# Attention, a dense MLP and eight routed experts on one core: blocks of 4, 3, 4, 4 and 3 tiles, and an order written out to the end

## The chip, the cores and the metric

One core of a Trainium2 chip. The time is that of one execution of the program on the device, in microseconds (us); lower is better. TensorE is called PE here, VectorE DVE, ScalarE ACT, GpSimd POOL, and SP is SyncE, whose queue issues most of the transfers.

## What is computed

2304 tokens of 512 numbers go through three stages:

```
# 1 attention inside chunks of 64 positions, 8 heads of 64
scores = scale * q_c @ k_c.T ; attn = softmax(scores) ; x = attn @ v_c
# 2 dense MLP, hidden size 2048
h = x @ w_in ; x = (h * clip(h + 3, 0, 6) / 6) @ w_out
# 3 eight experts, hidden size 1024, the two best by a noisy gate
noisy = x @ w_gate + log1p(exp(x @ w_noise)) * noise
top2, top2_w = two largest of noisy, softmax of the two
out[token] = sum over its two experts e:  top2_w * (relu(x @ w1[e]) @ w2[e])
```

Everything is float32. The products of stages 2 and 3 split each operand into a high and a low half and add three products (high by high, high by low, low by high), so every matmul of these stages stands three times.

## The kernel before

A tile is 128 tokens; there are 18. **Blocks.** Stage 2 goes through the tiles in five blocks (BT, 4, 4, 4, 3 and 3 tiles). A block does 16 units of 128 hidden columns. A unit is layer one (`s1`, 12 matmuls, L284, of 128 columns for each tile, into one of two banks), the activation (`mlp_act`: relu with bias on ACT L318, product on DVE L319, copy to the high half on ACT L320; then `mlp_lo`, the low half on DVE, L325), and layer two of the unit before (`mlp_o`, three matmuls, L293, for each tile, added up in one bank for each tile). So PE does layer one of unit u, then layer two of unit u - 1, while ACT and DVE make the halves of unit u.

**Ticks.** Every four matmuls of layer one and every tile of layer two count one tick. Work of other stages is put between matmuls by tick numbers or by unit (`at(...)`).

**Attention and gate beside the blocks.** Attention of block 0's tiles is done first, by itself. The tiles of block b + 1 are attended beside the units of block b: scores (`att_sc`, L187), exponentials, normalization (`att_n`, L225, or in block 0 by head on ACT, L230), transposes (`att_pt`, L237), their copy (`att_at`, L241), the product with the values (`att_xo`, L254), and its halves (`att_hi`, L264, `att_lo`, L267). In block 0 DVE and ACT also convert the MLP's weights from 64-bit words (`conv_1` to `conv_lo`, L152 to L175), two halves of a unit in each of 15 units. Its four attention tiles take four units each; the last is a hurried form (`fast`, three units), which normalizes on DVE. The gate for the tiles of block b - 1 runs beside block b: rows are written to memory, read back and transposed on DVE (L358), multiplied on PE (L399), transposed (L411) and reduced on DVE (L418); then come the best two (`gate_top`, four pieces, L436 to L470), positions in the experts' lists (`gate_pm`, L482, `gate_ps`, L499 to L503), and the scatter of each token's slot on POOL (L506).

**The last block.** For the gates of blocks 3 and 4, whose time is short, `route` uses PE for the transposes too (L382) and puts every step at a tick. Experts work in ten groups: expert 0 in two groups of 3 and 2 tiles, experts 1 to 6 with 5, expert 7 with 3 and 2. Their rows are found in a table (`exp_slots`, L517), gathered by POOL (L541, L557) and transposed: for expert 0 and 1 on PE (`exp_tr`, L567, halves by ACT L569 and DVE L570), later on DVE (`exp_tr_q`), for which the row numbers are worked out first (`exp_index`, DVE, L535, from tq, read from the table and copied three times). The weights of an expert unit are split on ACT and DVE (`split_unit`, L128, L129; called by `pump`, which also loads the unit three later). An expert unit is layer one, relu and low half (L583, L584), and layer two of the unit before (`exp_o`, L293). `exp_y` scales (L599 to L604) and POOL adds the rows to the output (L605). `counts` (L615 to L621) works out the longest list, which PE and others read into a register.

**What sets the order.** Inside `manual_schedule` an engine follows the order in which the program is written. This holds for PE, DVE and ACT up to the end of block 3 and from group 2 to the end; in the last block and groups 0 and 1 it holds for PE alone, and a scheduler places DVE and ACT's work; SP and POOL are placed by it throughout. The last `exp_o` and `exp_y` stand outside. Eight banks hold everything: four accumulators and two for layer one, and a pair, p6 and p7, for the rest (transposes, logits, gathered rows).

## Time and profile before

| | |
|---|---|
| median of 3 runs | 957.58 us (956.69 to 957.6) |
| the profiled execution | 958.57 us, of which the span is 956.8 |
| mean granted clock of PE | 0.989 of full speed |
| PE busy | 925.0 us, 97% of the span |
| DVE, ACT, POOL busy | 487.5, 339.5, 243.3 us (51, 35 and 25%) |

The span is the time from the first to the last instruction in the trace. PE is busy nearly throughout, so idle time of PE, its length and its releaser, is what to look for; busy shares of the other engines say little by themselves. The granted clock is the share of full speed that PE was given; below 1 the same matmuls take longer while PE still counts as busy.

### The profile page before, as it was taken

How to read it: one execution, taken by the hardware profiler on the slowest of the kernel's cores; microseconds unless marked ns; L12 is line 12 of the kernel's file. 1: busy time of each engine (PE TensorE's matmuls, PEld its weight loads, DVE VectorE, ACT ScalarE, POOL GpSimd, SP SyncE). 2: the span in 40 equal slices, each digit the busy share in tenths (PEclk: the TensorE clock that was granted, in tenths of full speed). 3: DMA queues.
4: the chain of work that ended last, by engine and by line, in shares of the span. 5: the costliest groups of instructions: out<-in, count | busy, mean ns of one | idle time of the engine just before them, and what ended most of it. 6: DMA issues, size and time to landing. Idle time of an engine off the chain costs nothing.

```text
span 956.8 us, 14478 instructions
## 1 busy us (share of the span) xinstructions
PE 925.0 (97%) x5810; PEld 785.3 (82%) x5810; DVE 487.5 (51%) x912; ACT 339.5 (35%) x658; POOL 243.3 (25%) x219
## 2 busy tenths in 40 slices
PE   7999899999999999999998999999999999999995
PEld 4677677777777888889987888998989999898894
DVE  6999954445444444555642554544545444441321
ACT  5566433233323333355531433333334333321210
POOL 0000000001100300033004474544746455432311
PEclk8999999999999999999999999999999999999998
DMA  9536431111841160035322753553636354140421
GB/s 348 192 103 207 167 99 55 34 34 51 272 162 34 34 186 2 1 79 164 112 98 57 177 148 116 122 127 95 146 119 133 117 115 127 62 58 20 56 33 26
DMA packets 50940, 102.67 MB, mean 107 GB/s; under 512 B 17200, under 2 KB 23728, under 8 KB 50864
## 3 DMA queue, kind: packets, MB, share of 16 engines
q1 hardware_dynamic: 39312, 80.64, 26.6%
q0 software_dynamic: 11552, 21.02, 11.8%
q8 instruction: 47, 0.77, 0.3%
q14 instruction: 29, 0.24, 0.1%
HBM read 78.31 MB, written 23.28 MB: 106 GB/s over the span
## 4 chain that ended last, share of the span: by engine, by line
PE 75%; DVE 11%; issue 7%; ACT 3%; DMA 2%; POOL 1%; SPq 0%; POOLq 0%; DVEq 0%; ACTq 0%
PE bp L284 36%; PE bp L293 32%; PE pair L293 4%; DVE u L161 2%; DVE u L153 2%; DVE r L319 1%; DVE g L325 1%; DVE w L175 1%; POOL table L506 1%; DVE u L152 1%; PE pair L254 1%; DMA table<-pay,slot 1%; PE pair L187 1%; ACT w L168 1%; PE pair L237 1%
## 5 line engine op out<-in xcount | busy, mean ns | idle before, releaser
L293 PE MATMUL bp<-w,g 128*128 128x512 f32 x1680 | 424.6, 398 | 0.0
L293 PEld LDWEIGHTS bp<-w,g 128*128 128x128 f32 x1680 | 310.4, 189 | 64.8 <-issue 0.8
L284 PE MATMUL bp<-Xa,w 128*128 128x320 f32 (+3 forms) x1344 | 249.0, 336 | 1.0 <-ACT w L168 1.0
L284 PEld LDWEIGHTS bp<-Xa,w 128*128 128x128 f32 x1344 | 215.9, 189 | 23.1 <-ACT w L168 1.8
L541 POOL DMA_INDIRECT xrq<-x2d,iq x120 | 131.7, 1097 | 105.2 <-DVE arena L358 40.3
L506 POOL DMA_INDIRECT table<-pay,slot x36 | 35.4, 982 | 457.7 <-DVE slot L503 448.2
L584 DVE SCALAR_TENSOR_TENSOR g<-bp,g 128x320 fp32r<-128x320 f32 (+2 forms) x128 | 62.8, 491 | 137.5 <-ACT g L583 137.5
L129 DVE TENSOR_TENSOR w<-raw,w 128x1024 fp32r<-128x1024 f32 x64 | 78.5, 1226 | 89.5 <-ACT w L128 89.3
L583 ACT ACTIVATE g<-bp 128x320 fp32r<-128x320 f32 (+2 forms) x128 | 56.0, 438 | 184.1 <-PE bp L284 184.0
L284 PE MATMUL bp<-Xe,w 128*128 128x320 f32 (+1 forms) x672 | 107.0, 314 | 1.0 <-ACT Xe L569 0.7
L284 PEld LDWEIGHTS bp<-Xe,w 128*128 128x128 f32 x672 | 103.5, 188 | 4.2 <-ACT Xe L569 0.9
L284 PE MATMUL bp<-Xb,w 128*128 128x384 f32 (+1 forms) x480 | 105.8, 366 | 0.0
L319 DVE SCALAR_TENSOR_TENSOR r<-r,bp 128x512 f32<-128x512 f32 (+1 forms) x80 | 50.7, 633 | 104.6 <-ACT r L318 104.4
L284 PEld LDWEIGHTS bp<-Xb,w 128*128 128x128 f32 x480 | 85.3, 188 | 12.4 <-issue 1.8
L318 ACT ACTIVATE r<-bp,b 128x512 f32<-128x512 f32 (+1 forms) x80 | 51.4, 642 | 120.8 <-PE bp L284 120.8
L605 POOL DMA_INDIRECT out_dram<-arena,tab x40 | 63.0, 1575 | 116.0 <-DVE arena L602 106.6
L128 ACT ACTIVATE w<-raw 128x1024 fp32r<-128x1024 f32 x64 | 67.8, 1060 | 64.1 <-PE pair L293 51.6
L325 DVE TENSOR_TENSOR g<-r,g 128x512 fp32r<-128x512 f32 (+1 forms) x80 | 51.0, 637 | 41.0 <-ACT g L320 40.9
L320 ACT ACTIVATE g<-r 128x512 fp32r<-128x512 f32 (+1 forms) x80 | 47.1, 589 | 57.1 <-DVE r L319 55.3
L293 PE MATMUL pair<-w,g 128*128 128x512 f32 x144 | 41.3, 395 | 0.0
L358 DVE STREAM_TRANSPOSE arena<-xrq 128x512 f32<-128x512 f32 x30 | 32.9, 1098 | 0.1
L293 PEld LDWEIGHTS pair<-w,g 128*128 128x128 f32 x144 | 27.0, 188 | 6.6
(151 smaller groups left out, 508.1 us busy)
## 6 DMA issues: line engine op xcount, KB each, us to landing
raw<-in_w2u_dram SPq DMA_DIRECT2D x64, 512.0 KB, 3.7
raw<-in_w1u_dram SPq DMA_DIRECT2D x24, 512.0 KB, 4.0
arena<-in_qkv_dram SPq DMA_DIRECT2D x14, 768.0 KB, 4.3
out_dram<-zero SPq DMA_DIRECT2D x4, 1536.0 KB, 18.5
rawx<-in_w1u_dram SPq DMA_DIRECT2D x8, 512.0 KB, 6.4
x2d<-x SPq DMA_DIRECT2D x15, 256.0 KB, 3.3
xq<-x2d SPq DMA_DIRECT2D x48, 64.0 KB, 3.2
xrq<-x2d,iq POOLq DMA_INDIRECT x120, 3.0
```

The source lines that it names most:

```text
L128: nc.scalar.activation(w[:, 0], raw, AF.Copy)
L129: nc.vector.tensor_tensor(w[:, 1], raw, w[:, 0].bitcast(F32), op=ALU.subtract)
L284: nc.tensor.matmul(dst, w[:, a, kd * P:(kd + 1) * P], x[:, b, kd, t0:t0 + n], start=(k == 0), stop=(k == 3 * KD - 1))
L293: nc.tensor.matmul(acc[i], g[:, a, i * P:(i + 1) * P], w[:, b, DM:], start=(first and j == 0), stop=(last and j == 2))
L318: nc.scalar.activation(r, st["h", b], AF.Relu, bias=b3)
L319: nc.vector.scalar_tensor_tensor(r, r, 6.0, st["h", b], op0=ALU.min, op1=ALU.mult)
L320: nc.scalar.activation(st["g", b, u][:, 0], r, AF.Copy)
L325: nc.vector.tensor_tensor(g[:, 1], st["r", b], g[:, 0].bitcast(F32), op=ALU.subtract)
L541: nc.gpsimd.indirect_dma_start(out=xr[:, c * P:(c + 1) * P], out_offset=None, in_=x2q, in_offset=bass.IndirectOffsetOnAxis(ap=st["iq", key ...
L583: nc.scalar.activation(g[:, 0, t0:t0 + n], h, AF.Relu)
L584: nc.vector.scalar_tensor_tensor(g[:, 1, t0:t0 + n], h, 0.0, g[:, 0, t0:t0 + n].bitcast(F32), op0=ALU.max, op1=ALU.subtract)
L605: s = nc.gpsimd.indirect_dma_start(out=out, out_offset=bass.IndirectOffsetOnAxis(ap=tab[:, i, 0:1], axis=0), in_=y, in_offset=None, comput ...
```

## The change

Block sizes become 4, 3, 4, 4 and 3. Beside block 0 three tiles are attended instead of four, so the hurried form goes; beside block 1, now three tiles wide, four. `att_at` is written ahead of `mlp_act`, and in blocks of three tiles the halves of attention go right behind layer one (list Z). The units of the gate's steps in blocks 1 to 3 change. The second-to-last gate (block 3) has four tiles, and `route` gets a loop for them, with `gate_top` in four pieces at four ticks, the positions of block 3 at tick 26 instead of 18 (17 instead of 16 for the last block), and products and transposes in p7 and p6 by turns. Rows of expert 0 are transposed from unit 11 of the last block on instead of 9; `exp_tr` uses p7 and p6 by turns, each now a tile of its own, since the pair's pool is closed after block 3. The order of DVE and ACT is as written from the last block to the end. The row numbers of expert 2 (`exp_index`) come in unit 0 of group 2 instead of unit 6 of group 1, and the gathers and transposes behind them are spaced anew. In the last group layer two of units 6 and 7 is done tile by tile (`exp_last`).

```diff
-BT = [4, 4, 4, 3, 3]
+BT = [4, 3, 4, 4, 3]
...
-        pt = bank("p7", [P, KD, P], "ptg")
+        pt = bank(("p7", "p6")[i % 2], [P, KD, P], "ptg")
...
+    def exp_last(key, e, nt):
+        for i in range(nt):
+            for u in (U2 - 2, U2 - 1):
+                g, w = st["g", key, u], st["w", e, u]
+                for j, (a, b) in enumerate(PASSES):
+                    nc.tensor.matmul(st["acc", key][i], g[:, a, i * P:(i + 1) * P], w[:, b, DM:],
+                                     start=False, stop=(u == U2 - 1 and j == 2))
...
-    EU = 9
+    EU = 11
...
             mlp_s1(b, u, gtile(), 0)
+            run(Z.get(u, []))
             mlp_act(b, u)
...
-                end = (B, u + 3)
+                end = (Z, u + 3)
...
-        for i in range(4):
+        for i in range(BT[1]):
...
+            if k == 3:
+                att_at(t, at_[0])
             mlp_act(0, u)
-            if k == 3 - fast:
-                att_at(t, at_[0])
...
-    def route(g, grp, rows, n0=16):
-
-        t = GRP[g][0]
-        steps = [(1, gate_t, t, "p5", 0), (2, gate_t, t + 1, "p6", 1), (3, gate_m, t, "p7"),
-                 (5, gate_r, t, "p7"), (5, gate_t, t + 2, "p5", 0), (5, gate_m, t + 1, "p7"),
-                 (7, gate_r, t + 1, "p7"), (7, gate_m, t + 2, "p7"), (9, gate_r, t + 2, "p7"),
-                 (9, gate_top, g), (n0, gate_pos, g), (n0, exp_slots, *grp)]
+    def route(g, grp, rows, n0=17, late=0):
+
+        t, nt = GRP[g]
+        steps = []
+        for i in range(nt):
+            steps += [(5 + 2 * i, gate_r, t + i, "p" + "76"[i % 2]), (3 + 2 * i, gate_m, t + i, "p" + "76"[i % 2]),
+                      (2 if i == 1 else 1 + 2 * i, gate_t, t + i, "p6" if i == 1 else "p5", i % 2)]
+        steps.sort(key=lambda x: (x[0], (gate_r, gate_t, gate_m).index(x[1])))
+        steps = [(n + late, *a) for n, *a in steps]
+        last = 3 + 2 * nt + late
+        d = (n0 - last) // 4
+        steps += [(last + i * d, gate_top, g, 1) for i in range(4)]
+        steps += [(n0, gate_pos, g), (n0, exp_slots, *grp)]
...
-        regular(1, {}, *between(1, (1, 4, 8, 12), (5, 7, 9, 11), 12))
+        regular(1, {}, *between(1, (1, 4, 8, 12), (3, 5, 7, 9), 11, 2))
...
-        regular(2, side, *between(2, (2, 6, 11), (3, 5, 7, 9), 10))
+        regular(2, side, *between(2, (1, 4, 8, 12), (5, 7, 9), 10, 2))
...
-        regular(3, side, *between(3, (2, 6, 10), (3, 5, 7, 9), 11))
-    order = tc.manual_schedule(engines={nc.tensor.engine})
+        regular(3, side, *between(3, (2, 6, 11), (3, 5, 7, 9), 10, 1))
+    heads.__exit__(None, None, None)
+    ends = ctx.enter_context(tc.tile_pool(name="ends", bufs=1, space=PSUM, side="right", reuse_waits="tile"))
+    single.update((tag, ends.tile([P, DM], F32, name="b" + tag)) for tag in ("p6", "p7"))
+    order = tc.manual_schedule(engines={nc.tensor.engine, nc.vector.engine, nc.scalar.engine})
...
-    at(side, 0, route, len(GRP) - 2, groups[0], NROW - BT[NB - 1] * P, 18)
+    at(side, 0, route, len(GRP) - 2, groups[0], NROW - BT[NB - 1] * P, 26, 3)
...
-            at(side, 6, exp_index, after[0])
+        elif gi == 2:
+            at(side, 0, exp_index, nxt_[0])
...
-            if u > 0:
+            if (gi, u) == (len(groups) - 1, U2 - 1):
+                exp_last(key, e, nt)
+            elif u > 0:
```

Where the order of an engine changes, the program's instruction lists show it. Names are the kernel's tiles; bp and pair are banks, and lines of the changed kernel are 2 to 10 higher. First ACT in the last block, from the first weight split on. Before:

```order
L318 ACTIVATE r<-bp_428,b_81 128x384
L437 ACTIVATE ns<-ns 128x24
L438 ACTIVATE ns<-ns 128x24
L320 ACTIVATE g<-r 128x384
L128 ACTIVATE w<-raw 128x1024
L463 ACTIVATE d<-d 128x3
L318 ACTIVATE r<-bp_427,b_81 128x384
L320 ACTIVATE g<-r 128x384
L128 ACTIVATE w<-raw 128x1024
```

And now:

```order
L128 ACTIVATE w<-raw 128x1024
L439 ACTIVATE ns<-ns 128x32
L440 ACTIVATE ns<-ns 128x32
L318 ACTIVATE r<-bp_427,b_81 128x384
L320 ACTIVATE g<-r 128x384
L128 ACTIVATE w<-raw 128x1024
L465 ACTIVATE d<-d 128x4
L318 ACTIVATE r<-bp_428,b_81 128x384
L320 ACTIVATE g<-r 128x384
```

The two exponential steps of the gate (ns) stood behind the relu (r) of a unit and now stand ahead of it; the one of d stood behind the second split as it does now.

Second, DVE in the same place. Before, from the difference of the best two (d) on:

```order
L462 TENSOR_TENSOR d<-mx_3745 128x3
L450 CAST ef<-ix_3746 128x2x3
L129 TENSOR_TENSOR w<-raw,w 128x1024
L453 TENSOR_TENSOR m_3755<-iota_82,ef 128x24 x2
L466 TENSOR_SCALAR s<-d 128x3
L319 SCALAR_TENSOR_TENSOR r<-r,bp_427 128x384
L456 TENSOR_TENSOR m<-m_3755 128x24
L467 RECIPROCAL s<-s 128x3
L458 TENSOR_TENSOR macc<-macc,m 128x8
L469 COPY pay<-s 128x3
L470 TENSOR_TENSOR pay<-s,d 128x3
L458 TENSOR_TENSOR macc<-macc,m 128x8 x2
```

And now, from the last search for the best two on:

```order
L448 MAX mx_3780<-ns 128x8
L449 MAX_INDEX ix_3781<-mx_3780,ns 128x8
L325 TENSOR_TENSOR g<-r,g 128x384
L129 TENSOR_TENSOR w<-raw,w 128x1024
L452 CAST ef<-ix_3781 128x2x4
L455 TENSOR_TENSOR m_3810<-iota_82,ef 128x32 x2
L458 TENSOR_TENSOR m<-m_3810 128x32
L460 TENSOR_TENSOR macc<-macc,m 128x8 x4
L464 TENSOR_TENSOR d<-mx_3780 128x4
L319 SCALAR_TENSOR_TENSOR r<-r,bp_428 128x384
```

The pieces of the gate (ef, m, macc, d) lay in twos and threes on both sides of the product (r) of a unit; now a piece stands whole between the weights' split and the next product, and the searches end ahead of the low half (g).

Third, DVE at the end of group 0. Before:

```order
L584 SCALAR_TENSOR_TENSOR g<-bp_428,g 128x384
L535 TENSOR_SCALAR iq<-tq,quarter 128x20
L584 SCALAR_TENSOR_TENSOR g<-bp_427,g 128x384
L570 TENSOR_TENSOR Xa<-pair_72,Xa 128x4x128 x2
L602 TENSOR_SCALAR arena<-bp_425,tab 128x512
```

And now:

```order
L586 SCALAR_TENSOR_TENSOR g<-bp_428,g 128x384
L586 SCALAR_TENSOR_TENSOR g<-bp_427,g 128x384
L572 TENSOR_TENSOR Xa<-bp_3593,Xa 128x4x128
L572 TENSOR_TENSOR Xa<-bp_3592,Xa 128x4x128
L612 TENSOR_SCALAR arena<-bp_425,tab 128x512
```

The row numbers (iq) stood ahead of the last activation of the group (g) and of the halves of the gathered rows (Xa); now nothing stands between them, and the two halves are read from two banks.

## Rows read from the trace of the kernel before

**Rows 1.** The page, part 1: engine, busy us (share of the span) and instructions.

```profile
PE 925.0 (97%) x5810; PEld 785.3 (82%) x5810; DVE 487.5 (51%) x912; ACT 339.5 (35%) x658; POOL 243.3 (25%) x219
```

**Rows 2.** PE's waits: PE, tile, line <- releaser: us in total, times, longest.

```profile
PE pair L567 <- DVE cnt L620: 1.4, 1, 1.4
...
PE bp L284 <- ACT Xe L569: 0.7, 1, 0.7
...
PE pair L399 <- DVE lgs L418: 0.6, 2, 0.3
```

**Rows 3.** Windows: length, busy us of each engine (instructions), granted PE clock, DMA share, GB/s.

```profile
101.94:130.77 28.83, 25.85 (x171) 20.46 (x165) 22.82 (x41) 13.52 (x34) 0.00 (x0) 0.94 0.39 128
...
118.02:121.60 3.58, 3.58 (x12) 3.02 (x13) 2.87 (x5) 0.63 (x1) 0.00 (x0) 0.62 0.00 0
...
521.50:523.00 1.50, 1.50 (x5) 1.13 (x4) 0.69 (x1) 0.21 (x1) 0.81 (x1) 0.50 0.04 3
...
539.67:541.66 1.99, 1.99 (x16) 1.99 (x17) 1.76 (x2) 0.79 (x2) 0.99 (x1) 1.00 0.87 329
```

**Rows 4.** Timeline of PE, block 0: start, us, line, operation, tiles [idle before <-releaser].

```profile
101.31 0.70 PE L254 MATMUL pair<-at,arena 64*64 64x64 f32 x32 [0.59 <-ACT at L241]
...
108.45 2.89 PE L284 MATMUL bp<-Xa,w 128*128 128x512 f32 x12
...
113.97 1.07 PE L284 MATMUL bp<-Xa,w 128*128 128x512 f32 x4
...
118.02 1.09 PE L237 MATMUL pair<-ident,arena 128*128 128x128 f32 x4 [2.98 <-DVE arena L225]
```

**Rows 5.** Timeline of PE, end of group 0.

```profile
515.77 0.75 PE L567 MATMUL pair<-ident,xr 128*128 128x128 f32 x4 [0.58 <-DMA xr<-x2d,tab]
...
519.95 1.13 PE L567 MATMUL pair<-ident,xr 128*128 128x128 f32 x4 [2.73 <-DVE Xa L570]
...
524.87 3.03 PE L284 MATMUL bp<-Xa,w 128*128 128x256 f32 x24
```

**Rows 6.** Timeline of DVE, block 0, the product of two successive units.

```profile
67.72 0.68 DVE L319 SCALAR_TENSOR_TENSOR r<-r,bp 128x512 f32<-128x512 f32 x1
...
73.76 0.68 DVE L319 SCALAR_TENSOR_TENSOR r<-r,bp 128x512 f32<-128x512 f32 x1
```

**Rows 7.** Timeline of PE, start of the last block.

```profile
410.38 0.86 PE L284 MATMUL bp<-Xa,w 128*128 128x384 f32 x4
...
422.70 2.27 PE L284 MATMUL bp<-Xa,w 128*128 128x384 f32 x12
```

**Rows 8.** Timeline of DVE, block 3: first and last rows of two gate pieces.

```profile
393.06 0.18 DVE L440 SCALAR_TENSOR_TENSOR ns<-lgs,ns 128x32 f32<-128x32 f32 x1
...
395.03 0.16 DVE L447 FIND_INDEX8 ix<-mx,ns 128x8 uint32<-128x8 f32 x1
...
398.64 0.16 DVE L450 CAST ef<-ix 128x8 f32<-128x8 uint32 x1
...
400.06 0.16 DVE L462 TENSOR_TENSOR d<-mx 128x4 f32<-128x4 f32 x1
```

**Rows 9.** Timeline of DVE, last block: product and low half of one unit.

```profile
430.02 0.56 DVE L319 SCALAR_TENSOR_TENSOR r<-r,bp 128x384 f32<-128x384 f32 x1 [0.52 <-ACT r L318]
...
431.17 0.56 DVE L325 TENSOR_TENSOR g<-r,g 128x384 fp32r<-128x384 f32 x1 [0.59 <-ACT g L320]
```

**Rows 10.** Timeline of DVE, end of group 0.

```profile
518.60 0.24 DVE L535 TENSOR_SCALAR iq<-tq,quarter 128x20 int32<-128x20 int32 x1 [7.15 <-DMA tq<-tq]
```

**Rows 11.** Timeline of PE, the last matmuls.

```profile
942.84 2.96 PE L293 MATMUL bp<-w,g 128*128 128x512 f32 x12
```

**Rows 12.** Timeline of POOL, the first of the two last scatters.

```profile
946.63 1.55 POOL L605 DMA_INDIRECT out_dram<-arena,tab  x1 [16.99 <-DVE arena L602]
```

**Rows 13.** Timeline of POOL, the last scatter of block 3's slots.

```profile
436.19 0.97 POOL L506 DMA_INDIRECT table<-pay,slot  x1 [0.30 <-issue]
```

**Rows 14.** Timeline of SP's queue, the read of the table behind it.

```profile
440.57 0.38 SPq L517 DMA_DIRECT2D tab<-table  x1
```

More of the change, by code (lines that the diff above doesn't have):

```diff
@@ L49, in tile_kernel @@
     dram = ctx.enter_context(tc.tile_pool(name="dram", bufs=1, space=DRAM))
-    ps = ctx.enter_context(tc.tile_pool(name="ps", bufs=1, space=PSUM))
     first = tc.tile_pool(name="first", bufs=1, space=PSUM)
     first_pool = first.__enter__()
-    pairs = [(first_pool if i else ps).tile([P, 2 * DM], F32, name=f"pair{i}") for i in range(4)]
+    heads = tc.tile_pool(name="heads", bufs=1, space=PSUM, side="right")
+    pairs = [(first_pool if i else heads.__enter__()).tile([P, 2 * DM], F32, name=f"pair{i}") for i in range(4)]
     single = {}
@@ L336, in x2_out @@
             t = B0[b] + i
-            if i > 2:
+            if b == NB - 2 and i > 2:
+                x2 = arena[:, i]
+            elif i > 2:
                 if extra is None:
@@ L749, in tile_kernel @@
     first.__exit__(None, None, None)
-    halves = ctx.enter_context(tc.tile_pool(name="halves", bufs=1, space=PSUM))
+    halves = ctx.enter_context(tc.tile_pool(name="halves", bufs=1, space=PSUM, reuse_waits="tile"))
     single.update((tag, halves.tile([P, DM], F32, name="b" + tag)) for tag, (i, j) in in_pair.items() if i)
@@ L760, in run, with regular @@
             f(*a)
-    EU = 9
+    EU = 11
     prev = []
-    def regular(b, side, A={}, B={}):
+    def regular(b, side, A={}, B={}, Z={}):
         nonlocal prev
@@ L783, in regular, with between @@
             prev = [(b, u)]
-    def between(b, attn, gates, top):
-        A, B, nt, n0 = {}, {}, BT[b], st.get("tick", 0)
+    def between(b, attn, gates, top, per):
+        A, B, Z, nt, n0 = {}, {}, {}, BT[b], st.get("tick", 0)
         before = BT[b - 1]
@@ L834, in between @@
         for i in range(4):
-            at(B, top + (i // 2 if b == 1 else i), gate_top, b - 1, 1)
-        pos, pm = (ENDS[1], top + 4 - (b == 1)) if nt > 3 else (bank("p5", [P, DM], "pos"), top + 4)
+            at(B, top + i // per, gate_top, b - 1, 1)
+        pos, pm = ENDS[1] if nt > 3 else bank("p5", [P, DM], "pos"), top + 5 - per
         s2_(pm, 1, gate_pm, b - 1, pos)
         at(B, pm, gate_ps, b - 1)
-        return A, B
+        return A, B, Z
     def block0():
@@ L863, in block0 @@
             prev = [(0, u)]
-            if not fast and k == 1:
+            if k == 1:
                 att_e(t, range(4, 8))
-            elif not fast and k == 2:
+            elif k == 2:
                 att_ns(t, range(4, 8))
@@ L875, in block0 @@
                 att_e(t, range(4))
-            elif k == 1 and fast:
-                att_n(t)
             elif k == 1:
@@ L887, in block0 @@
             conv_hi(a)
-            if fast and k == 0:
-                att_e(t, range(4, 8))
             conv_lo(b)
-            if k == 3 - fast:
+            if k == 3:
                 att_lo(t)
@@ L950, in tile_kernel @@
             at(side, 4, exp_slots_q, *after)
-            at(side, 6, exp_index, after[0])
+        elif gi == 2:
+            at(side, 0, exp_index, nxt_[0])
+            for i in range(nxt_[3]):
+                if i > 2:
+                    at(side, i, exp_tr_q, nxt_[0], i - 2)
+                at(side, i, exp_gather_q, nxt_[0], i)
+                if i == 1:
+                    at(side, 2, exp_tr_q, nxt_[0], 0)
+            at(side, 5, exp_tr_q, nxt_[0], 3)
+            at(side, 6, exp_tr_q, nxt_[0], 4)
+            at(side, 1, exp_slots_q, *after)
+            at(side, 5, exp_index, after[0])
             for i in range(3):
-                at(side, min(6 + i, 7), exp_gather_q, after[0], i)
-        elif gi > 1:
+                at(side, 5 + i, exp_gather_q, after[0], i)
+        elif gi > 2:
             if nxt_:
@@ L989, in tile_kernel @@
             late.__exit__(None, None, None)
-            X["b"] = ctx.enter_context(tc.tile_pool(name="xpool", bufs=1)).tile([P, 8 * CAP], F32R, name="Xe")
-        if gi == 1:
-            order.__exit__(None, None, None)
-            order = tc.manual_schedule(engines={nc.tensor.engine, nc.vector.engine, nc.scalar.engine})
-            order.__enter__()
+            X["b"] = ctx.enter_context(tc.tile_pool(name="xpool", bufs=1, reuse_waits="tile")).tile([P, 8 * CAP], F32R, name="Xe")
     order.__exit__(None, None, None)
-    exp_o(prevg[0], prevg[1], U2 - 1, prevg[2])
     exp_y(*prevg)
```

10 lines of the change are left out of this document (4 added, 6 removed).

## The prediction

> **What bounds the kernel now.** I read the page's busy times first: TensorE (PE) works 925.0 of 956.8 us, 97% [rows 1]. Its matmuls stay the same in number and nearly the same in columns (18 tiles through two layers, whatever block they lie in), so only three things can shorten the time: waits in front of PE, stretches at its lower clock, and what follows its last matmul. The second view is the list of PE's waits, which [rows 2] quotes in part. The third is the granted clock in short windows [rows 3], chosen by the longest waits in PE's timeline [rows 4, 5]: 0.62 in the 3.58 us behind a wait of 2.98, 0.50 behind one of 2.73, 1.00 behind the 1.43 on the counts. A window's share below 1.00 is a mixture of TensorE's two levels, 2.4 and 1.2 GHz, or the lower one all through (0.50). So each of the two long waits is paid twice, once as idle and once as slow matmuls behind it. What the reader should see: the engine is the bound nearly everywhere, and the gain is made of some ten places, each of which can be priced alone.
>
> **The change part by part.** All times are of the profiled execution.
>
> Block 0, fourth attention tile moved to block 1. A unit of four tiles takes PE 108.45 to 113.97, 5.52 us [rows 4]. Units 12 to 15 take 28.83 [rows 3]. In them stand the 2.98 wait for the normalized scores from VectorE (DVE) [rows 4] and the slow stretch, 3.58 x (1 - 0.62) = 1.4. Moved work is neither gain nor loss: three PE steps, one of 0.70 [rows 4] and two like it, 2.1. After the change these four units cost at best 4 x 5.52 = 22.1. But DVE converts weights there, and one unit of it without attention takes 67.72 to 73.76, 6.04 us [rows 6]. If DVE set the pace in three of the four units it would be 23.6. DVE's own attention work goes too, so it starts ahead, and following its steps by hand I get 22.6. The third wait for the copied scores, 0.59 at 101.31 [rows 4], goes because the copy is now written ahead of the activation; two earlier ones like it give little, since DVE at 6.04 a unit is behind anyway. So the gain is 28.83 - 22.6 - 2.1 + 0.59 = 4.7, with a tenth for the earlier two: **-4.8**, bounds -3.7 (23.6) to -5.2 (22.1).
>
> Block 1, now three tiles wide with four attention and four gate tiles: the steps come in a shorter unit, and the scores' first matmul can meet the low half still being written. Bound: nothing to one wait of the size at 101.31 [rows 4]. I take **+0.1**, since only one of the four tiles has the short interval. That DVE has more to do per unit is covered: no wait of PE on DVE stands in blocks 1 to 3 before. By the new order SyncE writes the zeros in this block, ahead of the rows of the fourth gate tile and of the next attention tiles; before, they stood in block 2 ahead of such rows and one such load, with no wait of PE in it, so they cost nothing unless the shorter units bring the need forward.
>
> Route of block 3, four tiles instead of three. PE goes from 410.38 to 422.70, 12.32 us [rows 7], for 24 matmuls of layer one and 18 of layer two, worth two units of 4.17, 8.4 (estimate from the 2.1 that twelve take there). The rest without the 0.32 wait is 3.6, 1.2 a tile. The tile is one less in the regular gates, which have two of its three PE steps (no transposes on PE). Bounds 0 to +1.2, taken **+0.5**.
>
> Last block, written order of DVE and ACT. Before, the scheduler spread the gate's arithmetic between the activations. Now four pieces stand whole: the second, in the like place of block 3, ran 393.06 to 395.19, 2.13, the third 398.64 to 400.22, 1.58 [rows 8]. The second stands ahead of the low half of unit 3, the third ahead of the product of unit 4; ACT's exponentials stand ahead of relu. An ordinary chain of a unit ends 431.73, 1.71 after the product starts at 430.02 [rows 9]; PE comes back for it one layer one and one layer two later, so about 1.8 of delay is free. Laying the pieces in, I get low half 3 late by 0.8, unit 4 by 1.1, then recovered: **+1.9**, bounds 0 (they fit in the free time) to +3.7 (both pieces in full). The weights' split, one per unit, already stands in such an order, and it costs nothing before.
>
> Gate banks alternate: the two 0.32 waits of the logits on the reduction [rows 2] go, **-0.6**, bound 0.
>
> End of group 0. From 515.77 to 524.87 PE has 8 transposes (1.0) and 15 matmuls of layer two (3.5) to do in 9.10, so 4.6 are lost, and 0.58 ahead of the first: 5.2 [rows 5]. The 2.73 was in truth not the transposed rows: DVE stood 7.15 on the row numbers of expert 2 [rows 10], with the activation and the copy of the first tile queued behind it. That instruction now comes in group 2, and the two transposes have a bank each. Next late is the gather, which already made the 0.58. It starts about 0.7 later, with gate positions one step later and behind the written activations, and PE arrives 0.4 earlier; so 1.6 there and 0.2 at the second tile. 5.2 - 1.8: **-3.4**, bounds -2.0 (the clock falls after the 1.6, at the 1.4 above) to -4.5.
>
> Counts: the 1.43 wait [rows 2] is PE's read of the largest count. In written order DVE makes it behind a weight split: **+0.6**, bounds -0.1 to +1.0.
>
> Start of group 2: the 0.69 wait on the transposed last tile [rows 2] gets half of a unit's layer one as cover: **-0.7**, bound 0, or -1.0 with what follows it.
>
> Tail: the last twelve matmuls start at 942.84 in 2.96, 0.23 apart [rows 11]; tile 0's last was the 11th and becomes the 6th, and its scaling and its scatter at 946.63 [rows 12] follow at once. 5 x 0.23 = 1.15; the second scatter needs the second tile just in time: **-1.1**, bound -0.7. The transposes of expert 0 from unit 11 on and the other moves lie beside matmuls and cost nothing while the gathers are early (rival 4).
>
> Sum: -4.8 + 0.1 + 0.5 + 1.9 - 0.6 - 3.4 + 0.6 - 0.7 - 1.1 = -7.5. From the profiled 958.57 that is 951.1; the median of the runs shown is 957.58, 1.0 lower, so 950.1, rounded to **950.0**. All bounds added give -12.6 to +0.1.
>
> **The rivals.**
> 1. The clock. Idle of 2.98 and 2.73 was followed by slow matmuls, idle of 1.43 by none [rows 2 to 5]; the new waits of about 1.6 and 2.0 lie between. If it falls behind both, each costs 1.4 like the stretch after 118.02: 950.0 + 2.8 = **952.8**. For: two of three waits did it. Against: the new ones are nearer to the one that did not. The Trainium skill says (TensorE: Matmul & The Clock Gate, HAM oscillation — how this bites in real kernels) that waits for data between bursts of matmuls can send the array back to its slow clock, so that the next burst starts cold. This trace agrees for its two long waits, 0.62 and 0.50, and disagrees for the 1.43, 1.00.
> 2. The written order in the last block costs nothing: the pieces of 2.13 and 1.58 fall into free time of 1.8 each. 950.0 - 1.9 = **948.1**. Against: 2.13 alone is more than 1.8, and the exponentials in front of relu add.
> 3. DVE takes over in block 0: three units at 6.04 [rows 6], and the copy's 0.59 gains nothing either: -3.1 instead of -4.8. **951.7**.
> 4. Slower: the slots of block 3 come late. Its positions are calculated eight steps later and behind the gate's pieces (together 8.6 by my working), and it has eight scatters instead of six, at 1.27 each 2.5 more. The read of the table, which followed the last scatter's start at 436.19 by 4.4, at 440.57 [rows 13, 14], so comes 11 later. On SyncE's queue weight loads stand behind it, and GpSimd's gathers of expert 0 wait for it. The first weight tile behind it is due at ACT's split in unit 10, six units behind the product at 430.02, so after some 6 us; the gathers have about 4 to spare, after two more units. Past that, ACT's split holds relu, and each us late is a us of PE. It decides at 4, and the kernel is slower than before from about 12 us of further delay. Against: no scatter or read of before takes a third of that. At 13 further: **959**.
>
> **How the numbers follow.** Chances: forecast 0.60, clock 0.14, no cost in the last block 0.12, DVE in block 0 0.08, late slots 0.06. The range, 946.0 to 954.6, takes in the second rival with the better bounds of block 0 and of group 0 (-1.5), and the clock with the worse bound of the last block (+1.8); beyond it I leave the late slots and the tails of the rest. A measurement of this kernel tells about 0.2%, 1.9 us, from no change, so faster means under 955.7. The forecast would have to lose 5.7 for that: faster 0.86, within 0.2% 0.08, slower 0.06.
>
> **What would show it.** Right: in block 0 no wait on the normalization and clock 1.00 in its last four units, which last under 23; no row-number instruction of DVE between the last activations of group 0; no wait of logits on the reduction; a wait of 1 to 2 on the gathered rows at the end of group 0, clock 1.00 behind it; a wait of about 2 on the counts; waits of about 1 on the low halves in the last block between 20 and 30 us after its start; the last scatter 1.1 sooner after the last matmul. Wrong: clock under 0.9 behind the gather or count waits; PE waiting on weights in unit 10 of the last block; PE waiting for a transfer in block 1, where SyncE now writes the zeros ahead of two loads; or block 0 with waits of PE on DVE in every unit.

## The result

The changed kernel takes 949.99 us, the median of four executions (948.82 to 951.32), against 957.59 for the kernel before on the same chip: ratio 0.9915, with a 95% interval of 0.9899 to 0.9931. The forecast was 950.0 in a range of 946.0 to 954.6. The profiled execution is one of the quicker ones, 948.82, with a span of 947.0 instead of 956.8.

The page, part 1, and PE's waits in the list by releaser (us in total, times, longest):

```profile
PE 921.0 (97%) x5814; PEld 780.9 (82%) x5814; DVE 489.1 (52%) x912; ACT 336.3 (36%) x644; POOL 242.0 (26%) x219
```

```profile
PE bp L569 <- DVE cnt L630: 1.5, 1, 1.5
...
PE bp L569 <- DMA xr<-x2d,tab: 1.3, 1, 1.3
...
PE bp L293 <- ACT g L320: 0.3, 1, 0.3
```

PE's busy time fell from 925.0 [rows 1] to 921.0, with four matmuls more (the transposes of one more gate tile): the granted clock was below 1 in the start, in block 0 and at the end of group 0, and is 1.00 there now. The count is still waited for, 1.46 instead of 1.43 [rows 2], and the logits no more. The granted clock in windows (the column behind POOL's) of the start of the changed kernel, of units 12 to 15 of block 0, and behind the two waits that are left:

```profile
0.00:23.90 23.90, 15.84 (x300) 8.97 (x301) 17.04 (x44) 11.81 (x44) 1.67 (x12) 1.00 0.92 343
...
101.03:123.54 22.51, 22.51 (x103) 17.97 (x97) 20.91 (x36) 9.49 (x16) 0.96 (x1) 1.00 0.40 133
...
514.32:517.20 2.88, 2.88 (x15) 2.34 (x14) 1.51 (x3) 1.10 (x2) 1.12 (x2) 1.00 0.56 156
...
532.04:535.43 3.39, 3.39 (x23) 3.13 (x24) 1.74 (x2) 1.82 (x3) 0.98 (x1) 1.00 0.56 199
```

In block 0 and group 0 it is 1.00 where [rows 3] had 0.94 and 0.50 (and 1.00 in the 2.04 us right behind the first of the two waits, from 512.28 on). The start of the kernel before, its first 24.98 us, had 0.86:

```profile
0.00:24.98 24.98, 18.18 (x300) 10.37 (x300) 16.90 (x44) 12.00 (x44) 1.67 (x12) 0.86 0.94 350
```

PE's timeline at the same places as [rows 4], [rows 7] and [rows 5], and the start of group 2:

```profile
100.41 0.69 PE L254 MATMUL pair<-at,arena 64*64 64x64 f32 x32
...
117.73 3.18 PE L284 MATMUL bp<-Xa,w 128*128 128x512 f32 x12
...
123.54 2.25 PE L284 MATMUL bp<-Xb,w 128*128 128x384 f32 x12
...
404.95 2.27 PE L284 MATMUL bp<-Xa,w 128*128 128x384 f32 x12
...
422.09 2.27 PE L284 MATMUL bp<-Xa,w 128*128 128x384 f32 x12
...
429.36 2.48 PE L293 MATMUL bp<-w,g 128*128 128x512 f32 x9 [0.33 <-ACT g L320]
...
512.28 0.75 PE L569 MATMUL bp<-ident,xr 128*128 128x128 f32 x4 [1.32 <-DMA xr<-x2d,tab]
...
513.82 0.75 PE L569 MATMUL bp<-ident,xr 128*128 128x128 f32 x4
...
517.20 3.03 PE L284 MATMUL bp<-Xa,w 128*128 128x256 f32 x24
...
542.42 3.76 PE L284 MATMUL bp<-Xe,w 128*128 128x320 f32 x24
```

No wait stands in front of the product at 100.41, and block 0 ends at 123.54 instead of 130.77. In the last block the only wait behind the gate pieces is one of 0.33 on the high half. At the end of group 0 the gathered rows are waited for, 1.32, and nothing else. DVE at that place, as [rows 10], then PE and POOL at the end, as [rows 11, 12]:

```profile
510.83 0.56 DVE L586 SCALAR_TENSOR_TENSOR g<-bp,g 128x384 fp32r<-128x384 f32 x1 [3.62 <-ACT g L585]
...
513.70 0.69 DVE L572 TENSOR_TENSOR Xa<-bp,Xa 128x512 fp32r<-128x512 f32 x1 [2.31 <-ACT Xa L571]
```

```profile
933.72 3.00 PE L594 MATMUL bp<-w,g 128*128 128x512 f32 x12
```

```profile
936.39 1.55 POOL L615 DMA_INDIRECT out_dram<-arena,tab  x1 [15.87 <-DVE arena L612]
```

DVE no longer stands on the row numbers. The first of the two last scatters starts 2.67 after the last twelve matmuls start, before 3.79; the last one 4.53 after them, before 5.65.

Since one execution differs from the next, I compare stages, as differences of starts in PE's timeline. A stage is named by where it begins: the first layer one of block 0, its first and third product of attention with the values, block 1, the second unit of the last block, group 0, group 1, group 2 (to group 3). "Again" are two more profiles of the kernel before (e11_before, e12_before, below) and one of the changed kernel (e7_again).

| | start | block 0 to 1st product | 1st to 3rd | 3rd to end | blocks 1 to 3 and a unit | last block | group 0 | group 1 | group 2 |
|---|---|---|---|---|---|---|---|---|---|
| before | 24.98 | 25.00 | 51.33 | 29.46 | 279.61 | 68.54 | 45.95 | 24.77 | 56.03 |
| before, again | 24.36 | 25.00 | 51.34 | 29.77 | 279.61 | 68.57 | 45.88 | 24.77 | 56.05 |
| before, again | 24.11 | 25.01 | 51.35 | 28.20 | 279.61 | 68.54 | 43.15 | 24.78 | 56.03 |
| changed | 23.90 | 24.26 | 52.25 | 23.13 | 281.41 | 70.20 | 42.05 | 25.22 | 54.12 |
| changed, again | 24.35 | 24.24 | 52.23 | 23.15 | 281.40 | 70.16 | 42.01 | 25.22 | 54.12 |

Groups 3 to 9 take the same, within 0.05. A stage repeats within 0.05 in most places; where it doesn't (end of block 0 and group 0 of the kernel before), the clock or a transfer differs, and the experiment on why the kernel before spreads is on that.

### The profile page after: what moved, and what is told of

Same layout as the page of the kernel before. It is cut to its first block, busy times and chain, and to the rows that moved or that the text cites. A ratio compares the mean times of both kernels' runs of the same rounds, so it can differ in the third digit from the quotient of the medians.

```text
span 947.0 us, 14446 instructions
## 1 busy us (share of the span) xinstructions
PE 921.0 (97%) x5814; PEld 780.9 (82%) x5814; DVE 489.1 (52%) x912; ACT 336.3 (36%) x644; POOL 242.0 (26%) x219
## 5 line engine op out<-in xcount | busy, mean ns | idle before, releaser
L293 PE MATMUL bp<-w,g 128*128 128x512 f32 x1812 | 455.1, 397 | 0.4 <-ACT g L320 0.3
L293 PEld LDWEIGHTS bp<-w,g 128*128 128x128 f32 x1812 | 333.5, 188 | 71.7 <-DVE g L325 0.8
L284 PEld LDWEIGHTS bp<-Xb,w 128*128 128x128 f32 x480 | 85.3, 188 | 12.6 <-issue 1.8
L168 ACT ACTIVATE w<-u 128x512 fp32r<-128x512 f32 x32 | 20.2, 633 | 32.5 <-DVE u L161 32.5
```

The source lines that it names most:

```text
L284: nc.tensor.matmul(dst, w[:, a, kd * P:(kd + 1) * P], x[:, b, kd, t0:t0 + n], start=(k == 0), stop=(k == 3 * KD - 1))
L293: nc.tensor.matmul(acc[i], g[:, a, i * P:(i + 1) * P], w[:, b, DM:], start=(first and j == 0), stop=(last and j == 2))
```

## The experiments

Chips differ: on two of the four that ran these, PE, ACT and DVE have idle time that the profile puts down to "issue" or "remote", that is to nothing that it shows of this core. It delays PE between 565 and 587 us in every kernel profiled there, and near 205 us in most; I call it issue waits, and its cause is not known. Times are therefore compared with the kernel before, or with the changed kernel, of the same chip, and stages outside those places.

**The row numbers alone (e3_index).** The kernel before, with this:

```diff
-            at(side, 6, exp_index, after[0])
-            for i in range(3):
-                at(side, min(6 + i, 7), exp_gather_q, after[0], i)
+        elif gi == 2:
+            at(side, 0, exp_index, nxt_[0])
...
```

> The kernel before with one part of the change alone: the row numbers of expert 2, and the gathers and transposes behind them, come in group 2 instead of group 1. If DVE's 7.15 wait on them was the cause of PE's 2.73 wait and of the slow clock behind it (1.4), the time falls by 4.1 from 957.6 to 953.5, and PE waits only for the gather (0.6). If the transposes' single bank was the cause, the 2.73 becomes a wait of about 1 to 2 on the copy of the first tile, and the gain is 1 to 2.

PE's timeline at the end of group 0:

```profile
522.24 0.75 PE L567 MATMUL pair<-ident,xr 128*128 128x128 f32 x4 [0.22 <-DMA xr<-x2d,tab]
...
524.40 0.75 PE L567 MATMUL pair<-ident,xr 128*128 128x128 f32 x4 [0.71 <-DVE Xa L570]
```

The 2.73 is now 0.71 on the copy of the first tile, the gather costs 0.22, and the clock stays at 1.00. The stage of group 0 takes 42.04, against the change's 42.05; the near equality is chance, since the waits in the two differ (0.71, 0.22 and one of 0.32 on the logits here, 1.32 there). The time, 967.4 against 962.0 on that chip where 4.1 less was expected, says nothing on this: it holds two waits of 1.9 and 1.7 in the last block behind an ACT that started 2.3 late (its releaser is given as remote), and 4.8 of issue waits near 580. So the cause is shown in its stage, the 4.1 in the time are not. The 0.71 is the single bank, which the next run isolates.

**One bank again (e8_bank).** The changed kernel, with this:

```diff
-        pt = bank(("p7", "p6")[i % 2], [P, KD, P], "ptg")
+        pt = bank("p7", [P, KD, P], "ptg")
...
-            steps += [(5 + 2 * i, gate_r, t + i, "p" + "76"[i % 2]), (3 + 2 * i, gate_m, t + i, "p" + "76"[i % 2]),
+            steps += [(5 + 2 * i, gate_r, t + i, "p7"), (3 + 2 * i, gate_m, t + i, "p7"),
```

> The changed kernel with the logits and the gathered rows in one bank again, as before. Each gate product then waits for the reduction of the tile before (0.32 before the change, one or two times in each of two routes), and the second transposes at the end of group 0 wait for the halves of the first, about 0.6. Against the changed kernel of the same group 1.3 to 1.9 higher. If the banks don't matter, it is the same within 0.3, and the waits that went had another cause.

PE's timeline at the route of block 3 and at the end of group 0:

```profile
413.68 0.42 PE L401 MATMUL bp<-at,wg_sb 128*32 128x128 f32 x8 [0.56 <-DVE lgs L420]
...
418.85 0.43 PE L401 MATMUL bp<-at,wg_sb 128*32 128x128 f32 x8 [0.32 <-DVE lgs L420]
...
514.14 0.75 PE L569 MATMUL bp<-ident,xr 128*128 128x128 f32 x4 [1.26 <-DMA xr<-x2d,tab]
...
516.29 0.75 PE L569 MATMUL bp<-ident,xr 128*128 128x128 f32 x4 [0.70 <-DVE Xa L572]
```

951.51 against 949.29 of e7_again, on the same chip: 2.2 higher, above the 1.3 to 1.9 expected. The last block is 1.2 longer and group 0 1.0. So the banks are worth more than the 0.6 that I gave them; the waits of the logits come back in front of the gate's products (0.56, 0.32 and, in group 0, 0.31), and one of 0.70 in front of the second transposes.

**The changed kernel again (e7_again).**

> The changed kernel as it is, beside the others of this group and against the kernel before on the same chip. On the chip of the last group the kernel before took 958.9 to 966.3 with PE, ACT and DVE waiting for the issue of instructions near 205 and 570 us; none of that is in the two profiles first compared. Theory: the gain is in the stages, so here too the changed kernel is 7 to 10 lower, a ratio of 0.990 to 0.993, whatever the level. Rival: part of the 7.6 was the first chip's; then the ratio is above 0.994. If its times fall into two groups again, the profile's stage lengths say where, against 24.3, 52.3, 23.1 (block 0), 79.4, 98.4, 95.9, 42.1, 25.2, 54.1.

949.29 (948.61 to 950.89) against 955.62 (953.16 to 958.45): 0.9928, 0.9914 to 0.9942. A gain of 6.3: the ratio is inside the 0.990 to 0.993 expected, the gain below the 7 to 10; the interval overlaps the first. Its stages repeat; the kernel before is quicker on this chip, and its 17 executions spread over 5 us.

**Why the kernel before spreads (e11_before, e12_before).** No edit.

> The kernel before as it is, for another profile of it. In the one first read, the 2.73 wait at the end of group 0 was followed by PE at a clock of 0.50, and the stage from group 0 to group 1 took 45.95; in the run with the copy alone, whose program is the same there, a wait of 2.38 was followed by 1.00 and the stage took 43.78. Theory: whether the clock falls behind that wait differs from execution to execution, so the stage is near 44 in one profile and near 46 in another, and some 1.4 of my 3.4 there was that execution's and not the kernel's; block 0's fourth tile (2.98, followed by 0.62) is the same each time, 29.4 to 29.6 for its last stage. Rival: the clock falls behind the 2.73 each time and 43.78 came of the shorter wait.

> The kernel before once more, same question as the run beside it: the stage from group 0 to group 1 near 44 (clock 1.00 behind the wait) or near 46 (0.50), the last stage of block 0 at 29.4 to 29.6 either way.

PE's timeline of the first, at the wait on the normalization in block 0 and at the end of group 0, and windows behind the two:

```profile
117.42 0.63 PE L237 MATMUL pair<-ident,arena 128*128 128x128 f32 x4 [3.04 <-DVE arena L225]
...
519.60 0.75 PE L567 MATMUL pair<-ident,xr 128*128 128x128 f32 x4 [2.38 <-DVE Xa L570]
```

```profile
117.42:121.00 3.58, 3.58 (x12) 2.92 (x13) 2.87 (x5) 0.63 (x1) 0.00 (x0) 0.61 0.00 0
...
521.50:523.00 1.50, 1.50 (x5) 1.13 (x5) 0.87 (x2) 0.00 (x0) 0.07 (x1) 0.50 0.42 108
```

The same two views of the second:

```profile
117.19 0.63 PE L237 MATMUL pair<-ident,arena 128*128 128x128 f32 x4 [3.04 <-DVE arena L225]
...
516.58 0.75 PE L567 MATMUL pair<-ident,xr 128*128 128x128 f32 x4 [1.69 <-DVE Xa L570]
```

```profile
117.19:120.80 3.61, 3.61 (x18) 3.04 (x19) 3.19 (x6) 1.32 (x2) 0.00 (x0) 1.00 0.00 0
...
518.50:519.97 1.47, 1.47 (x8) 1.16 (x7) 0.94 (x2) 0.49 (x1) 0.22 (x2) 1.00 0.49 103
```

The idle in block 0 is 3.04 in both; behind it PE had 0.61 in one and 1.00 in the other. So I was wrong that block 0's stage is the same each time: 29.77 and 28.20. At the end of group 0 the wait itself differs, 2.38 and 1.69 (the copies of tq land earlier or later), and the clock behind it, 0.50 and 1.00; 45.88 and 43.15. In the run with the copy alone (below) a wait of 2.38 was followed by 1.00, so the length of the wait alone doesn't decide it. The two executions took 958.13 and 953.89, and the two places differ by 1.57 and 2.73, which is all of the 4.2 between them. The rule that I weighed (the Trainium skill, TensorE: Matmul & The Clock Gate, HAM oscillation — how this bites in real kernels: waits between bursts can send the array back to the slow clock) is seen in one of these executions (0.61 and 0.50) and not in the other (1.00 twice). The two places explain the difference between these two executions, and the profile from which I predicted was one that paid at both.

**The copy alone (e4_copy).** The kernel before, with this:

```diff
-            mlp_act(0, u)
             if k == 3 - fast:
                 att_at(t, at_[0])
+            mlp_act(0, u)
```

> The kernel before with one line moved: in block 0 the copy of the transposed scores is written ahead of the unit's activation. It takes away PE's wait of 0.59 in front of the product with the values, three times. My prediction: DVE sets the pace at 6.04 a unit, so only the first (DVE is not yet behind) and the third count; the stage from the first product to the third becomes longer, 52.3 instead of 51.3, and all in all at most 0.7 is gained. Rival: PE sets the pace, all three count, and 1.8 is gained.

PE's timeline in block 0, and the window behind the wait at the end of group 0 that was spoken of above:

```profile
43.09 0.33 PE L237 MATMUL pair<-ident,arena 128*128 128x128 f32 x1 [0.79 <-ACT arena L230]
...
95.34 0.33 PE L237 MATMUL pair<-ident,arena 128*128 128x128 f32 x1 [0.79 <-ACT arena L230]
...
118.56 0.76 PE L237 MATMUL pair<-ident,arena 128*128 128x128 f32 x4 [3.89 <-DVE arena L225]
...
520.11 0.75 PE L567 MATMUL pair<-ident,xr 128*128 128x128 f32 x4 [2.38 <-DVE Xa L570]
```

```profile
520.11:521.60 1.49, 1.49 (x8) 1.34 (x9) 0.08 (x1) 0.60 (x1) 0.47 (x1) 1.00 0.28 10
```

Slower, where a gain of up to 0.7 was expected: 958.02 against 955.62, 1.0028 (1.0013 to 1.0042). The stages of block 0 are 24.31, 52.27 and 30.89: the first two are those of the changed kernel to 0.05, so the wait on the copy (0.59, three times) only turned into one in front of the transposes (0.79 at all three tiles, where it was 0.79, 0.15 and 0.20), and the fourth tile's wait grew from 2.98 to 3.89 (granted clock 0.55 in the 3.44 us behind it). Block 0 takes 107.47, against 104.56 to 106.11 in the three profiles of the kernel before. That DVE sets the pace there held; that the third wait would count in full did not.

**The copy behind again (e9_behind)**, in the best kernel below:

```diff
-            if k == 3:
-                att_at(t, at_[0])
             mlp_act(0, u)
+            if k == 3:
+                att_at(t, at_[0])
```

> The best kernel so far (945.1 on the last chip; later transposes, count read at the end, scheduler in the last block and group 0) with the copy of the transposed scores in block 0 behind the unit's activation again. The run with that line moved alone was slower than the kernel before. Theory: DVE sets the pace in block 0, so the line only moves PE's waits from the product to the transposes; the three stages of block 0 become 25.0, 51.3 and about 23.4 against 24.2, 52.2 and 23.2, the same sum within 0.3. Rival: the copy ahead is itself the loss (it delays the activation on ACT and with it DVE), then the sum falls by 0.8 or more.

951.74 against 962.31 on a third chip (0.9896, 0.9868 to 0.9924), with issue waits. The stages of block 0 are 24.93, 51.34 and 22.86 against 24.23, 52.24 and 23.15 of e6_best: 0.5 less. Between the two expectations: the copy ahead is a small loss in the changed kernel too, not the gain of 0.6 in my sum. The run also isolates the moved tile: with the copy where it was, the first two stages are those of the kernel before (25.00 and 51.33), so that the third, 22.86 against 28.20 to 29.77, is shorter by the fourth tile alone.

**Half of the conversion on GpSimd (e10_pool)**, in the same kernel:

```diff
-        nc.vector.tensor_tensor(lo, st.pop(("u", s)).bitcast(F32), hi.bitcast(F32), op=ALU.subtract)
+        eng = nc.gpsimd if s > 3 and s % 2 == 0 else nc.vector
+        eng.tensor_tensor(lo, st.pop(("u", s)).bitcast(F32), hi.bitcast(F32), op=ALU.subtract)
```

> The best kernel so far with every second low half of the converted weights (14 subtractions of 128x512) on GpSimd instead of DVE, which has nothing to do in block 0. It takes 0.74 a unit off DVE. Theory: DVE is what sets the 26.1 of four units with an attention tile, PE needs 22.1 + 2.0; so each falls by 1.5 to 2.0, the stage between the first and the third product from 52.2 to 48.5 to 49.5, and all of block 0 by 4 to 6, if GpSimd keeps up and DVE's own instructions stay as long. Rival: the two engines slow each other down in memory or GpSimd takes longer than a unit (5.5), DVE's instructions grow beyond their 0.68, and block 0 stays or becomes longer.

Timelines in block 0, of POOL, of PE and of DVE:

```profile
66.46 1.29 POOL L176 TENSOR_TENSOR w<-u,w 128x512 fp32r<-128x512 f32 x1 [5.02 <-ACT w L168]
```

```profile
67.81 0.73 PE L285 MATMUL bp<-Xa,w 128*128 128x512 f32 x2 [0.20 <-POOL w L176]
```

```profile
85.00 0.69 DVE L176 TENSOR_TENSOR w<-u,w 128x512 fp32r<-128x512 f32 x1
...
86.36 0.69 DVE L320 SCALAR_TENSOR_TENSOR r<-r,bp 128x512 f32<-128x512 f32 x1 [0.67 <-ACT r L319]
```

It missed: block 0 is 99.0 instead of the 99.6 of e6_best, where 4 to 6 less was expected. The time, 952.64 in the median of three executions on the same chip as the run above, has no run of e6_best there to stand against. DVE now has idle time (0.67 in front of a product), so it was relieved. DVE's instructions that ran beside GpSimd's 14 are products and halves of attention, which read one operand from a bank and stay at 0.68 to 0.69, and conversion steps with one operand, which take 0.42 to 0.46 there and once 1.33, where they take 0.42 in the changed kernel. So the engines do slow each other a little; none of DVE's instructions with both operands outside the banks ran beside GpSimd's, so whether those grow is not shown. But GpSimd takes 1.29 for what DVE does in 0.69, starts when ACT's high half is there, and PE waits for it (0.20 here, 0.20 to 0.64 at five places). ACT's high half in turn waits for DVE's word (u), and ACT's relu, for which DVE idles, stands behind that half. These waits point to that chain as what sets the pace of 25.7 for four units with a tile; no run isolates it. So "DVE sets the pace" was true of the kernel before, and only just: a second limit lies 0.4 a tile behind it. The fourth execution took 1504 us, at a mean granted clock of 0.557 where the others had 0.993 to 0.996; why, I don't know.

**Written order or scheduler (e2_sched).** The changed kernel, with this, and the switch to the written order for all three engines again behind group 1:

```diff
-    order = tc.manual_schedule(engines={nc.tensor.engine, nc.vector.engine, nc.scalar.engine})
+    order = tc.manual_schedule(engines={nc.tensor.engine})
```

> The changed kernel with DVE and ACT placed by the scheduler again in the last block and in groups 0 and 1, PE as written. My prediction charged the written order with 1.9 in the last block and 0.6 at the counts; the traces show some 1.1 and 0. If the written order is a loss there, PE has no wait on the high half in the last block and the time is about 1 lower (947.8 in its faster runs). Rival: the written order is what removed waits at the start of group 2 (0.69 and 0.31) and brought the gather no later; then it is 1 or more higher, 949.8 and above.

PE's timeline at the end of group 0 and at the start of group 2:

```profile
514.65 0.75 PE L569 MATMUL bp<-ident,xr 128*128 128x128 f32 x4 [0.78 <-DMA xr<-x2d,tab]
...
547.37 1.89 PE L284 MATMUL bp<-Xe,w 128*128 128x320 f32 x11 [0.63 <-DVE Xe L572]
```

The last block takes 69.64 instead of 70.20 and no wait stands in it; group 0 takes 41.51, the gather 0.78 instead of 1.32, since the slots come earlier. At the start of group 2 a wait of 0.63 is back. So each expectation held in its place: the written order costs 0.6 in the last block (1.0 by e6_best, below) and 0.5 at the gather, and gains 0.6 at group 2. The time is 958.89 against 961.96, on a chip with issue waits, which hide differences of this size.

**Filling the waits (e1_fill).** The changed kernel, with this:

```diff
+                at(ticks, st["tick"] + 1, fill, "p7", 5)
                 at(ticks, st["tick"] + 1, exp_tr, groups[1][0], 0)
...
+        fill("p6", 6)
         st["most"] = nc.values_load(cnt[0:1, NE:], min_val=0, max_val=RGN)
```

> The changed kernel with matmuls on a matrix of ones, whose result nobody reads, put on PE ahead of the two longest waits that are left: five (about 1.1 us) ahead of the first transposes at the end of group 0, six (about 1.3 us) ahead of the read of the counts. Its four runs so far are two at 948.8 (mean granted clock 0.996) and two at 951.2 (0.992 and 0.994). Theory: in the slower two the clock fell behind one of these waits; then every run here is at 948.8 to 949.2 with a clock of 0.996. Rival: the clock falls at another place (start of the program, block 0); then runs near 951 with 0.992 to 0.994 stay about as frequent.

PE's timeline at the end of group 0, and ACT's later on:

```profile
512.42 1.25 PE L567 MATMUL bp<-ones 128*128 128x512 bf16 x5
...
513.94 0.75 PE L574 MATMUL bp<-ident,xr 128*128 128x128 f32 x4 [0.26 <-DMA xr<-x2d,tab]
```

```profile
568.70 0.44 ACT L590 ACTIVATE g<-bp 128x320 fp32r<-128x320 f32 x1 [4.23 <-remote]
...
576.52 0.44 ACT L590 ACTIVATE g<-bp 128x320 fp32r<-128x320 f32 x1 [7.39 <-remote]
```

Inconclusive. The time is 959.05 against 961.96, 0.997. The fillers stand in the waits and the stages are as long as without them (42.20, 25.21). But this chip adds issue waits, ACT alone 7.39 at a stretch, and the twelve executions run from 957.2 to 961.4. Why two of the first four executions of the changed kernel took 2.3 more, at a clock of 0.992 and 0.994 instead of 0.996, stays open: the profiles of it (two, and e8_bank) show 1.00 behind its waits of 0.7 to 1.6. The rival has one profile for it. In e5_late, whose program is the same up to the end of group 0, the clock fell in the start:

```profile
0.00:25.68 25.68, 18.41 (x300) 10.38 (x301) 18.14 (x46) 12.26 (x45) 1.67 (x12) 0.87 0.93 346
```

That start is 1.3 longer than in e7_again (24.35, at 1.00). The longest wait of PE between 9 and 24 us is as long in both, 1.63 and 1.62, so a wait of this size too was followed by either clock. Whether the two slower executions paid there, no profile shows.

**The waits that are left (e5_late, e6_best).** e5_late moves the transposes and the read of the count; e6_best adds the scheduler for the last block and group 0.

```diff
-                at(ticks, st["tick"] + 1, exp_tr, groups[1][0], 0)
-                at(ticks, st["tick"] + 2, exp_tr, groups[1][0], 1)
+                at(ticks, st["tick"] + 3, exp_tr, groups[1][0], 0)
+                at(ticks, st["tick"] + 4, exp_tr, groups[1][0], 1)
...
-        st["most"] = nc.values_load(cnt[0:1, NE:], min_val=0, max_val=RGN)
...
+    st["most"] = nc.values_load(cnt[0:1, NE:], min_val=0, max_val=RGN)
     order.__exit__(None, None, None)
     exp_y(*prevg)
```

> The changed kernel with two further moves: the two transposes at the end of group 0 stand two matmul groups later (after the third and fourth tile of layer two instead of the first and second, 1.4 us of work ahead of them), and the longest count is read into registers at the end of the program instead of in group 1. Theory: both waits go, 1.32 less 0.3 for halves that come nearer to their use, and 1.46, so the faster runs are at 946.3; and if these waits were where the clock fell, all runs are there. Rival: the read of the count has a price at the end of the program, up to 1, and the halves of the second tile are late by 0.5 or more; then it is 948 or above.

> The changed kernel with the later transposes at the end of group 0, the count read at the end, and DVE and ACT placed by the scheduler in the last block and group 0 (written from group 1 on). Against the changed kernel of the same group: the stage from group 0 to group 1 loses the 1.0 that it lost with the later transposes alone, group 1 loses 1.4, the last block 0.6: 3.0 lower, about 0.3%. Rival: where the scheduler's stretch ends, DVE and ACT are placed worse, as at the start of group 2 with the scheduler to there (0.6 waited); then 2.0 to 2.4 lower.

PE's timeline of e6_best at the end of group 0, where no wait is left:

```profile
511.53 0.63 PE L569 MATMUL bp<-ident,xr 128*128 128x128 f32 x4
...
512.74 0.75 PE L569 MATMUL bp<-ident,xr 128*128 128x128 f32 x4
...
514.73 3.18 PE L284 MATMUL bp<-Xa,w 128*128 128x256 f32 x24
```

e5_late: group 0 takes 41.04 (1.0 less) and group 1 23.80 (1.4 less), as expected, with 0.40 of the wait on the gather left; the rival's price at the end of the program isn't there. Its time (957.45 against 961.96) was again on the chip with issue waits. e6_best: 945.05 (944.41 to 946.66), 4.2 lower than e7_again on the same chip, where 3.0 was expected (the last block gave 1.0 and group 0 1.8), and 0.9887 (0.9870 to 0.9904) of the kernel before. Group 0 takes 40.25, the last block 69.16, and group 2 keeps its 54.12. It beats both kernels.

## Why the prediction was right, step by step

**The sum.** It was made against the profiled execution, 7.5 below its 958.57. Profile against profile the fall is 9.8, 2.3 more; on the medians it is 7.6 on one chip and 6.3 on another. Against e12_before, a profile with the clock at 1.00 in the start, block 0 and group 0, the span is only 5.1 shorter (952.1 and 947.0). So part of the 7.5, and of the 7.6, belongs to executions that paid; that 950.0 meets 949.99 is closer than the steps are, and in so far luck: errors of 0.6 to 0.9 in four steps (block 0, last block, counts, start of group 2) partly cancelled.

**Block 0**, forecast -4.8. Its three stages fell by 6.15, and the moved tile gives 2.1 of it to the next blocks: -4.1. The last four units went to 22.5, as followed by hand (22.6). The 0.59 did not come; the copy ahead is worth about +0.2 over the first three tiles (24.26 + 52.25 against 25.00 + 51.33). And 1.3 to 1.6 of the stage is the clock, which the kernel before pays in some executions only; without it the gain is 2.8 (104.56 less 99.64 less 2.1).

**Blocks 1 to 3 and the route**, forecast 2.1 (moved) + 0.1 + 0.5, of which the route's new tile falls into the next stage. The stage of blocks 1 to 3 grew by 1.80; the wait of attention is 0.35 in one place, inside its bounds. The zeros on SyncE's queue in block 1 delayed nothing that PE waited for.

**Last block**, the step that failed most in size. The stage grew by 1.66. With the scheduler it grew by 1.10 (e2_sched, on a chip with issue waits) and by 0.62 (e6_best); so the written order costs 0.6 to 1.0, and not 1.9, and the new tile, with the wait on the logits that went, 0.6 to 1.1. The second gate piece did stand ahead of the low half, which ended at 424.81, but PE had already begun on the high half, and its nine matmuls from 424.20 took 2.56 instead of 2.26: 0.3, where I had 0.8. Then came the 0.33 on the next unit, behind which layer two started 0.50 late and took 0.21 longer: 0.7, where I had 1.1. Together that is the 1.0 of e6_best. The rival with no cost here was wrong as well; the truth lay between.

**Banks**, forecast -0.6: the two waits of 0.32 went, but taking the banks back costs 2.2 (e8_bank). The alternate banks also remove 0.70 in front of the second transposes, which I had counted with the row numbers, and a logit wait of 0.56 that the kernel before didn't have.

**End of group 0**, forecast -3.4 and -0.3 of the banks: -3.90 in the profiles, by the cause named (e3_index). But the 5.2 that I took for the loss was that execution's; in another the stage takes 43.15, and the gain is 1.1. It was also too large: the same 8 transposes and 15 matmuls take 4.92 without a wait (512.28 to 517.20), not 4.5, so 4.8 were lost. The wait forecast on the gather, 1.6 and 0.2, is 1.32, 0.5 less; the two errors cancel.

**Counts**, forecast +0.6, measured 0.03 in the wait: DVE made the counts as early in the written order. **Start of group 2**, forecast -0.7: the stage is 1.9 shorter, 0.4 of it a transpose that moved to group 1; both waits (0.69 and 0.31) went, and the scheduler brings one back (e2_sched); the 0.5 that is left is not attributed. **Tail**, forecast -1.1: 1.12, up to the last scatter. From there to the end the profiles of both kernels vary between 8.1 and 9.1, so the whole tail of this pair is 0.7 shorter.

**The start** of the program, before any change, gave 1.1 between the two profiles. It belongs to neither kernel, and here too the clock makes the difference: in three of the fourteen profiles it takes 24.98 to 25.68 at a granted clock of 0.86 to 0.88 (before, e3_index, e5_late), in the other eleven 23.90 to 24.36 at 1.00. So the profile from which I predicted paid at three places, and I saw two of them.

**The rivals.** The clock did not fall behind the new waits in any profile; it was 1.00 where the old waits had been. The start shows that this is no proof for every execution. The bounds added give -12.5 at the lower end, not -12.6. The late slots of block 3 did not come: the table was read 10.7 later than before, counted from the start of group 0 (447.49 to 475.15 against 440.57 to 478.92), as worked out (11), and PE waited for neither weights nor rows in the last block.

## What to carry to other kernels

Before a stall is priced from one profile, a second profile of the same kernel tells which part of it comes back: here two places differed by 4.3 us between executions, and the start by up to 1.8. Compare stages between fixed instructions, not end times; they repeat within 0.05 us where the end repeats within 5. And an instruction that waits for a transfer on an in-order engine costs what stands behind it: look at who waits for that engine next, as with the row numbers that held back a copy of quite another tile.

## What was not expected of the hardware

The same idle of 3.04 us in front of the same matmuls was followed by the full clock in one execution and by 0.61 in another, and one of 2.38 by 1.00 (e4_copy) and by 0.50 (e11_before). The start of the program ran at a granted clock of 0.86 to 0.88 in three profiles and at 1.00 in eleven, and in e5_late it fell although no wait of PE from 9 us on was longer than 1.63. A subtraction of 128x512 took 1.29 us on GpSimd and 0.69 on DVE; beside it DVE's steps with one operand took up to 0.46 and once 1.33 instead of 0.42 (e10_pool). On two of the chips the engines idled up to 7.4 us, put down to issue or remote, at the same two places of the program, which the other two never showed.
